# Attention and a feed-forward layer on one core: the last span's second product in two levels of Strassen

## Chip, core and metric

The kernel runs on one core of a Trainium2 chip. The metric is device time in microseconds (us). It is the median of three runs; the profile comes from one further execution of the same kernel. TensorE is called PE in the profile, VectorE DVE, ScalarE ACT, GpSimd POOL, and SyncE, which only issues transfers here, SP.

## What is computed

Cut to what matters:

```python
def reference(q, k, v, g_q, g_k, w_in, w_out):      # q, k, v: 8 x 12 x 448 x 64
    q_n, k_n = rmsnorm(q, g_q), rmsnorm(k, g_k)
    attn = softmax(q_n @ k_n.T / 8)                  # per batch and head
    x = (attn @ v), heads side by side               # 3584 x 768
    h = x @ w_in                                     # 768 x 2048
    g = np.maximum(h, 0.0) ** 2
    return g @ w_out                                 # 2048 x 768, result 3584 x 768
```

The change lies in the last line alone, and there in its last quarter of tokens.

## The kernel before

The 3584 tokens are worked off in four spans (`NSPAN = 4`) of 896 tokens, two batches of `S = 448` each. For every span the kernel does the attention, then a first product (x by w_in, then the squared ReLU), then a second product (by w_out). Both products use one level of Strassen's method in Winograd's form: operands are cut into 2 x 2 blocks, and seven block products (named A11, S2, S1, S3, A12, A22, S4 after their weight operand) take the place of eight. The seven weight operands of each product are made once, at the start, and kept in device memory as `w1s` and `w2s`. The sums of activations are `xC` (from `xT`) for the first product and `gC` (from `gT`) for the second; `combine` (L1021 to L1032) makes the latter on DVE.

`first_product` (L1034) goes over `HF = 8` row blocks f of w_in's columns, and for each over the seven block products. One block product is three matmul statements of 128 x 128 weights by 128 x 448 activations (L1068). Four PSUM tiles receive them: `pa` (from the pool `ps_s`), and `pb`, `pc`, `pd` from the function `bank` (L460), which hands out two PSUM banks "m" and "n" in turn, by a counter `turn`. DVE adds L1075 (z), L1078 (y) and L1083 (into `gT`) and the ACT and POOL steps L1040 and L1044 empty them.

`second_product` (L1091) goes over `HC = 3` column blocks m and the seven block products i, in the order of `uses2` (L642). One block product is eight matmul statements of 128 x 448 (L1134). Results leave by `deliver` (L1102): a DVE transpose in 32 x 32 squares (L1104), then four transfers (L1107). The very last block product is done by `last_block` (L1109), in two halves of 224 columns (L1119), so that the end of the kernel is short. Before each second product `turn` is moved on by one, so that its first bank is not the one that the first product has used last.

Weights come as a stream. `load_blocks(upto)` (L651) issues one transfer for each weight block on the SP queue (L665), into five buffers `sw`; it is called with "my index + 5", so up to four blocks lie ahead of the one in use. A block of the first product has 192 KB and serves 3 matmul statements; a block of the second product has 256 KB and serves 4. The stream runs on across the products and spans. SP does its issues in program order, and waits in that order too: for a buffer to become free, and, at `deliver`, for DVE's transpose.

The order of each engine's work is the order of the program text; it is written out by hand (`manual_schedule`), and there is no planner. In the spans before the last, the attention of the next span is woven into the second product. In the last span there is no attention left: first product and second product follow each other, with nothing else on PE.

In the profile every float32 matmul statement shows as two weight loads and two matmul records.

Of the kernel before, what the change touches and what calls it, by code (L numbers as in the profile page):

```python
# [10 lines left out]
F32 = mybir.dt.float32  # L11
U32 = mybir.dt.uint32
AF = mybir.ActivationFunctionType
ALU = mybir.AluOpType
# [373 lines left out]
def attention_then_ffn_bounded(  # L388
# [47 lines left out]
    HF = NFC // 2  # L436
    NSPAN = B // 2
# [7 lines left out]
    def start_of(span):  # L445
        return 2 * span * NPAIR
# [8 lines left out]
    ps_s = ctx.enter_context(tc.tile_pool(name="ps_s", bufs=2, space=bass.MemoryType.PSUM))  # L455
    ps_o = ctx.enter_context(tc.tile_pool(name="ps_o", bufs=1, space=bass.MemoryType.PSUM))
# [29 lines left out]
    HW = HC * P  # L486
# [153 lines left out]
    stream = []  # L640

    uses2 = [(m, i) for m in range(HC) for i in (A11, A12)]  # L642
    uses2 += [(m, i) for m in range(HC) for i in (S2, S1, S3, A22, S4)]
    def order_of(span, f):

        return (A11, A12, S2, S1, S3, A22, S4) if span == f == 0 else range(7)

    N1 = HF * 7
    N2 = HC * 7 * (HF // 4)

    def load_blocks(upto):  # L651

        while len(stream) < min(upto, NSPAN * (N1 + N2)):
            n = len(stream) % (N1 + N2)
            if written[0] < min(2 * (n // 7 + 1) if n < N1 else 2 * NFC, 2 * NFC):
                return
            sw = loads.tile([P, 4, P], F32, tag="sw", name="sw", bufs=5)
            if n < N1:
                sw = sw[:, 0:HC]
                src = w1s[n // 7, order_of(len(stream) // (N1 + N2), n // 7)[n % 7]].rearrange("p (c m) -> p c m", c=HC)  # L660
            else:
                n -= N1
                m, i = uses2[n // (HF // 4)]
                src = w2s[i, n % (HF // 4), :, :, m * P:(m + 1) * P]
            nc.sync.dma_start(sw, src)  # L665
            stream.append(sw)
# [4 lines left out]
    places, halves, rests = [], [], {}  # L671
# [419 lines left out]
    def second_product(work, span):  # L1091

        B11, B21, B22 = gT[:, 0:HF, 0:S], gT[:, HF:, 0:S], gT[:, HF:, S:2 * S]
        T1, T2, T4, T3 = gC[:, 0], gC[:, 1], gC[:, 2], gT[:, 0:HF, S:2 * S]
        rhs_of = {A11: B11, S2: T2, S1: T1, S3: T3, A12: B21, A22: T4, S4: B22}
        rows = out.rearrange("(b g t) n -> b t g n", b=B, t=32)
        n = span * (N1 + N2) + N1
        add = nc.vector.tensor_tensor
        done = []
        turn[0] += 1  # L1100

        def deliver(ct, col, t, queues=(nc.sync,), part=slice(0, S // 32)):  # L1102
            osb = work.tile([P, S // 32, 32], F32, tag="osb", name="osb")[:, part]
            nc.vector.transpose(osb.rearrange("p g n -> p (g n)"), ct[:, part.start * 32:part.stop * 32])  # L1104
            for i in range(0, P, 32):
                queue = queues[i // 32 % len(queues)]
                queue.dma_start(rows[2 * span + t, :, part, col * P + i:col * P + i + 32], osb[i:i + 32])  # L1107

        def last_block(n, m):  # L1109

            deliver(*done.pop(), (nc.sync, nc.scalar))
            load_blocks(n + 5)
            rhs = rhs_of[S4]
            ct = work.tile([P, S], F32, tag="ct", name="ct", bufs=1)
            half = S // 64 * 32
            for part in (slice(0, half), slice(half, S)):
                ps = bank("ps")[:, part]
                for c in range(HF):
                    nc.tensor.matmul(ps, stream[n + c // 4][:, c % 4], rhs[:, c, part],  # L1119
                                     start=c == 0, stop=c == HF - 1)  # L1120
                add(ct[:, part], y[:, part], ps, ALU.add)
                deliver(ct, m, 1, (nc.sync, nc.scalar), slice(part.start // 32, part.stop // 32))

        p1s, c11s = {}, {}
        for j, (m, i) in enumerate(uses2):
            if span == NSPAN - 1 and j == len(uses2) - 1:
                last_block(n, m)
                break  # L1130
            ps = bank("ps")
            for c in range(HF):
                load_blocks(n + 5)
                nc.tensor.matmul(ps, stream[n][:, c % 4], rhs_of[i][:, c], start=c == 0, stop=c == HF - 1)  # L1134
                n += c % 4 == 3
                if c == HF // 2 - 1 and done:
                    yield
                    deliver(*done.pop())
                if span == 0 and j < 8 and c % 4 == 1:
                    combine(j % 4 * HF // 4 + c // 4, (j // 4,))  # L1140
                if c < HF - 1:
                    yield
            if i == A11:
                p1s[m] = work.tile([P, S], F32, tag="p1", name="p1", bufs=HC)
                nc.scalar.copy(p1s[m], ps)
            elif i == S2:
                add(p1s[m], p1s[m], ps, ALU.add)
            elif i == S1:
                y = work.tile([P, S], F32, tag="y", name="y", bufs=1)
                add(y, p1s[m], ps, ALU.add)  # L1150
            else:
                ct = work.tile([P, S], F32, tag="ct", name="ct", bufs=1)
                add(ct, p1s[m] if i in (A12, A22) else y, ps, ALU.add)
                if i == S3:
                    add(p1s[m], p1s[m], ps, ALU.add)
                done.append((ct, m + (HC if i in (S3, A22) else 0), 1 if i in (S3, S4) else 0))
            yield
        if done:
            deliver(*done.pop())
            yield  # L1160


    load_v(0)

    def ahead(u, nxt):

        if u == 7 * (HF - 3):
            norm(nxt)
        if u == 7 * (HF - 2):
            norm(nxt + 1)  # L1170
            load(nxt + 2)
        if u == 7 * (HF - 1):
            transposes(nxt)
            squares(nxt + 2)

    with tc.tile_pool(name="words", bufs=2) as spare["pool"]:
# [20 lines left out]
        with tc.tile_pool(name="first_product", bufs=2, reuse_waits="tile") as work:  # L1197
            for u, _ in enumerate(first_product(work, 0)):
                if u == 6:

                    left = ps_s.tile([P, 2, 512], F32, tag="s", name="bits")
# [4 lines left out]
                if u == N1 - 4:  # L1206
                    transposes(NAT)
                    squares(NAT + 2)
    for span in range(NSPAN):
        more = span + 1 < NSPAN  # L1210
        nxt = start_of(span + 1)
        if span:
            with tc.tile_pool(name="first_product", bufs=2, reuse_waits="tile") as work:
                for u, _ in enumerate(first_product(work, span)):
                    if more:
                        ahead(u, nxt)
        with tc.tile_pool(name="second_product", bufs=2, reuse_waits="tile") as work:
            rest = second_product(work, span)
            if more:
                places_for(work, NJ)  # L1220
                places.append(qkT[:, 1])
                halves[:] = [work.tile([P, 2, S // 2], F32, tag=f"half{m}", name="half", bufs=1) for m in range(2)]
                sums_for(work)
                total, done, most = HC * (7 * HF + 4) - 20, 0, 10 * NPAIR + 1
                for u, _ in enumerate(attention(nxt)):
                    while done < total * min(u + 1, most) // most + 3 * max(u + 1 - most, 0):
                        next(rest)
                        done += 1
            for _ in rest:
                pass  # L1230


@with_exitstack
# [85 lines left out]
```

## Time and profile before

| what | value |
|---|---|
| median of three runs | 1363.46 us (1362.93 to 1364.74) |
| the profiled execution's own time | 1362.31 us |
| span of the profiled execution, first to last instruction | 1360.5 us |
| mean granted clock of TensorE | 0.997 |
| busy: PE, DVE, POOL, ACT | 1340.5, 832.1, 566.0, 430.0 us |
| last span: first product on PE | from 1101.5 to 1227.8 us |
| last span: second product on PE | from 1227.8 to 1354.3 us |

The profile has a page of summaries and views of the trace: groups of instructions (count, busy time, mean duration, idle time before them and what ended it), the chain of work that ended last, a timeline of one stretch, a table by windows, and, for one source line, the time from a transfer's issue to its landing. In a timeline, records that follow each other with the same names are merged, and their number stands as "x6"; times are from the span's start.

### The profile page before, as it was taken

Reading aid. Unit: us, or ns where it says so; the run is one execution under the profiler, and the core shown is the slowest. Engines: PE = TensorE matmul, PEld = TensorE weight load, DVE = VectorE, ACT = ScalarE, POOL = GpSimd, SP = SyncE. Lnnn points to the kernel's source line nnn. Section 1 sums busy time; section 2 is a strip of 40 time slices with the busy share of each in tenths; the row PEclk is TensorE's granted clock in tenths of the full one; section 3 lists DMA queues with packets and bytes.
Section 4 is the critical chain, followed back from the end, with each engine's and each line's share of the span. In section 5 each row is a group of like instructions: output and inputs, shape, how many; then the busy total and the mean of one; then the engine's idle time right before and its main releaser. Section 6 shows DMA issues by size and latency. Waiting matters only on the chain.

```text
span 1360.5 us, 16880 instructions
## 1 busy us (share of the span) xinstructions
PE 1340.5 (99%) x5618; PEld 641.6 (47%) x5618; DVE 832.1 (61%) x1482; ACT 430.0 (32%) x674; POOL 566.0 (42%) x458
## 2 busy tenths in 40 slices
PE   8999999999999999999999999999999999999998
PEld 3333445444444455444444455444444455555554
DVE  6999788599987333467778523557788633332111
ACT  7886466433332011233332111233333211110000
POOL 5667533466563122655565222446566312220000
PEclk9999999999999999999999999999999999999999
DMA  9777999655685333355675433345765443334443
GB/s 240 208 229 198 314 360 327 183 130 111 130 151 129 99 87 88 100 119 118 135 150 115 113 100 87 101 104 118 142 129 110 105 103 87 87 91 107 106 111 71
DMA packets 434084, 190.12 MB, mean 140 GB/s; under 512 B 282948, under 2 KB 430788, under 8 KB 433988
## 3 DMA queue, kind: packets, MB, share of 16 engines
q1 hardware_dynamic: 427364, 180.33, 52.2%
q0 software_dynamic: 4736, 8.40, 2.5%
q8 instruction: 47, 0.77, 0.2%
q10 hardware_dynamic: 1888, 0.23, 0.1%
q14 instruction: 49, 0.40, 0.1%
HBM read 155.72 MB, written 33.16 MB: 139 GB/s over the span
## 4 chain that ended last, share of the span: by engine, by line
PE 90%; DVE 5%; ACT 3%; DMA 1%; issue 1%; SPq 0%; POOL 0%; ACTq 0%; DVEq 0%
PE ps L1134 37%; PE pd L1068 10%; PE pa L1068 10%; PE pc L1068 10%; PE sc L785 7%; PE pav L862 7%; PE pb L1068 5%; ACT gT L797 1%; DVE gT L810 1%; DVE rstd L715 1%; PE sc L793 1%; DVE gC L613 1%; PE tot L876 1%; DMA gT<-in_moe_w_in_dram 1%; PE pav L851 1%
## 5 line engine op out<-in xcount | busy, mean ns | idle before, releaser
L1134 PE MATMUL ps<-gT,sw 128*128 128x448 f32 x752 | 293.0, 543 | 0.0
L1134 PE MATMUL ps<-gC,sw 128*128 128x448 f32 x576 | 225.2, 543 | 0.0
L1044 POOL TENSOR_TENSOR gT<-gT 128x448 f32<-128x448 f32 x96 | 93.9, 980 | 283.3 <-ACT gT L1040 283.3
L1134 PEld LDWEIGHTS ps<-gT,sw 128*128 128x128 f32 x752 | 141.1, 190 | 146.4 <-issue 142.0
L750 POOL TENSOR_TENSOR half<-half,mhalf 128x28 f32<-128x28 f32 x36 | 175.2, 4868 | 72.7 <-DVE half L749 69.2
L1134 PEld LDWEIGHTS ps<-gC,sw 128*128 128x128 f32 x576 | 108.1, 190 | 112.9 <-issue 110.7
L1068 PE MATMUL pa<-xT,sw 128*128 128x448 f32 x384 | 155.0, 540 | 0.6 <-ACT p L1072 0.6
L1040 ACT ACTIVATE gT<-gT 128x448 f32<-128x448 f32 x96 | 55.3, 577 | 311.2 <-DVE gT L1083 311.2
L787 ACT ACTIVATE pr<-sc 128x896 f32<-128x896 f32 x87 | 77.5, 915 | 121.7 <-PE sc L785 121.7
L785 PE MATMUL sc<-qkT 64*64 64x448 f32 (+1 forms) x1152 | 109.8, 496 | 0.0
L1068 PEld LDWEIGHTS pa<-xT,sw 128*128 128x128 f32 x384 | 72.9, 190 | 72.6 <-issue 70.7
L583 POOL TENSOR_TENSOR gC<-gC 128x384 f32<-128x384 f32 x64 | 76.2, 1209 | 62.2 <-DVE gC L579 60.4
L1083 DVE TENSOR_TENSOR gT<-z,pd 128x448 f32<-128x448 f32 x32 | 19.8, 620 | 97.8 <-PE pd L1068 97.6
L1068 PE MATMUL pd<-xT,sw 128*128 128x448 f32 x192 | 77.9, 542 | 1.3 <-DVE z L1075 1.3
L1068 PE MATMUL pd<-xC,sw 128*128 128x448 f32 x192 | 77.5, 540 | 1.3 <-DVE gT L1083 1.3
L1068 PE MATMUL pb<-xC,sw 128*128 128x448 f32 x192 | 77.5, 540 | 0.1
L752 POOL TENSOR_TENSOR qk<-qk,half 128x448 f32<-128x448 f32 x72 | 76.4, 1081 | 2.8
L1068 PE MATMUL pc<-xC,sw 128*128 128x448 f32 x192 | 77.4, 539 | 0.0
L1068 PE MATMUL pc<-xT,sw 128*128 128x448 f32 x192 | 77.4, 539 | 0.0
L830 POOL DMA_DIRECT2D xT<-factors x72 | 38.0, 532 | 94.7 <-DMA factors<-square 63.9
L862 PE MATMUL pav<-pr,vt 64*64 64x448 f32 x348 | 72.7, 537 | 0.0
L862 PE MATMUL rest<-pr,vt 64*64 64x448 f32 x348 | 72.7, 537 | 0.0
(144 smaller groups left out, 1849.6 us busy)
## 6 DMA issues: line engine op xcount, KB each, us to landing
sw<-w1s SPq DMA_DIRECT2D x224, 192.0 KB, 2.4
sw<-w2s SPq DMA_DIRECT2D x168, 256.0 KB, 3.2
w1s<-gC SPq DMA_DIRECT2D x8, 1344.0 KB, 6.4
w2s<-gC SPq DMA_DIRECT2D x8, 1344.0 KB, 6.1
out_dram<-osb SPq DMA_DIRECT2D x186, 56.0 KB, 1.9
qk<-in_q_dram SPq DMA_DIRECT2D x144, 56.0 KB, 3.5
qk<-in_k_dram SPq DMA_DIRECT2D x144, 56.0 KB, 3.0
xT<-factors POOLq DMA_DIRECT2D x72, 112.0 KB, 3.4
```

The lines of the kernel that those rows point to most:

```text
L583: nc.gpsimd.tensor_tensor(*[blocks_of(n)[:, place_of(n, i)] for i in (dst, x, y)], op)
L750: nc.gpsimd.tensor_tensor(half, half, mhalf, ALU.pow)
L752: nc.gpsimd.tensor_tensor(qkn[:, s], raw[:, s], half[:, s * NG:(s + 1) * NG].rearrange("p g -> p g ()").to_broadcast([P, NG, 32]), ALU.mult)
L785: nc.tensor.matmul(sc[part, h, 0:n], qkT[rows, 0, 1, keys], qkT[rows, 0, 0, of], start=True, stop=True)
L787: nc.scalar.activation(pr, sc[:, :, 0:n], AF.Exp)
L830: nc.gpsimd.dma_start(xT[h * D:(h + 1) * D, b % 2, hp], sums["out"][i % 2].rearrange("(h g) t -> h () (g t)", h=2)[h].to_broadcast([D, S]))
L862: nc.tensor.matmul(into, vs[i][rows, h, c, :], probs[i, c][rows, h, :], start=(c == 0), stop=(c == NF), skip_group_check=True)
L1040: nc.scalar.activation(g, src, AF.Relu)
L1044: nc.gpsimd.tensor_tensor(g, g, g, ALU.mult)
L1068: nc.tensor.matmul(ps, stream[n + at][:, c], rhs[:, c], start=first and c == 0, stop=c == HC - 1, skip_group_check=not first)
L1083: add(g, x, ps, ALU.add)
L1134: nc.tensor.matmul(ps, stream[n][:, c % 4], rhs_of[i][:, c], start=c == 0, stop=c == HF - 1)
```

## The change

The first three spans are as before. The last span's second product is done by a new function, `last_product`, that

- goes over the seven block products in the order A11, A12, S2, S1, S3, A22, S4 on the outside, and treats all three column blocks of one before it goes to the next;
- cuts each of them for the column blocks m = 0 and 1 (of both halves of the result: four of its six) once more into 2 x 2 parts, and does seven inner block products of four matmul statements each, 128 x 128 by 128 x 224; the third column block stays with eight statements of 128 x 448 (`third`);
- gets the sums of weight parts from GpSimd (`add_weights`: four additions of 128 x 512 for each outer step) and the sums of activations from DVE (`add_g`: four subtractions of 128 x 896);
- adds the inner results up by `meet` (DVE, 128 x 224) and `based` (GpSimd, 128 x 224, which adds to z and y what the result already holds);
- loads the weights of one outer step by one transfer of 1536 KB into one of two places (`load_set`): the first two at the start of the last span, the others at the end of each step. The stream of small blocks ends with the last span's first product;
- keeps its sums in places whose contents are no longer needed (`qk`, `qkT`, `xT`, `xC`, and parts of `gT`), and one new tile `wb`;
- does not move `turn` on before it begins.

`deliver` is moved out of `second_product`; `last_block` is gone, and the last `third` is done in two halves in its place.

The core of the diff:

```diff
-        while len(stream) < min(upto, NSPAN * (N1 + N2)):
+        while len(stream) < min(upto, NSPAN * (N1 + N2) - N2):
...
+        def load_set(o):
+            if o < len(order):
+                nc.sync.dma_start(sets[o % 2].rearrange("p (k e) -> p k e", k=2),
+                                  w2s[order[o]].rearrange("k p c m -> p k (c m)"))
...
+            for dst, x, y, op in ((s1, a21, a22, add), (s2, s1, a11, sub), (s3, a11, a21, sub), (s4, a12, s2, sub)):
+                nc.gpsimd.tensor_tensor(dst, x, y, op)
...
+            dst, x, y = ((t1, b12, b11), (t2, b22, t1), (t3, b22, b12), (t4, b21, t2))[n]
+            nc.vector.tensor_tensor(dst, x, y, sub)
...
+        def run(ps, lhs, rhs, first=True):
+            for c in range(HK):
+                nc.tensor.matmul(ps, lhs[:, c], rhs[:, c], start=first and c == 0, stop=c == HK - 1,
+                                 skip_group_check=not first)
...
+            into = {A11: [(None, p1s)], A12: [(p1s, None)], S2: [(p1s, p1s)], S1: [(p1s, ys)],
+                    S3: [(ys, None), (p1s, p1s)], A22: [(p1s, None)], S4: [(ys, None)]}[i]
...
+            def third():
+                m = HC - 1
+                for part in (slice(0, HS), slice(HS, S)) if end else (slice(0, S),):
+                    ps = bank("ps")[:, part]
+                    for c in range(HF):
+                        nc.tensor.matmul(ps, weights_of(o, m, c // HK)[:, c % HK], rhs_of[i][:, c, part],
+                                         start=c == 0, stop=c == HF - 1)
...
+                if not end:
+                    add_g(o + 1, 0)
+                    send(m)
...
+            pa = ps_s.tile([P, 2, 512], F32, tag="s", name="pa")[:, 0, 0:HS]
+            run(pa, a11, b11)
+            p1 = small_of("p1i")
+            nc.scalar.copy(p1, pa)
+            if not end:
+                third()
+            pb = ps_o.tile([P, S], F32, tag="o", name="pb")[:, 0:HS]
+            run(pb, s2, t2)
+            z, y = small_of("zi"), small_of("yi")
+            nc.vector.tensor_tensor(z, p1, pb, add)
+            z21, z12 = based(1, 0, z, "za"), based(0, 1, z, "zb")
+            pc = bank("pc")[:, 0:HS]
+            run(pc, s1, t1)
+            nc.vector.tensor_tensor(y, z, pc, add)
+            add_g(o + 1, 1)
+            y22 = based(1, 1, y, "yb")
+            pd = ps_o.tile([P, S], F32, tag="t", name="pd")[:, 0:HS]
+            run(pd, s3, t3)
+            meet(1, 1, y22, pd)
+            run(pa, a12, b21, False)
...
+            add_g(o + 1, 2)
+            run(pd, a22, t4, False)
+            meet(1, 0, z21, pd)
+            send(1)
+            run(pc, s4, b22, False)
+            meet(0, 1, z12, pc)
+            send(0)
+            add_g(o + 1, 3)
+            load_set(o + 2)
+            add_weights(o + 1)
+            if end:
+                third()
...
+        load_set(0)
+        load_set(1)
+        with tc.tile_pool(name="first_product", bufs=2, reuse_waits="tile") as work:
+            for u, _ in enumerate(first_product(work, NSPAN - 1)):
+                if u == N1 // 2:
+                    add_weights(0)
+                if u == N1 - 2:
+                    for n in range(4):
+                        add_g(0, n)
+        with tc.tile_pool(name="second_product", bufs=2, reuse_waits="tile") as work:
+            rest.send(work)
```

More of the change, by code (lines that the diff above doesn't have):

```diff
@@ L1095, in second_product @@
         rhs_of = {A11: B11, S2: T2, S1: T1, S3: T3, A12: B21, A22: T4, S4: B22}
-        rows = out.rearrange("(b g t) n -> b t g n", b=B, t=32)
         n = span * (N1 + N2) + N1
@@ L1100, in second_product @@
         turn[0] += 1
[L1102 to L1126, printed above, removed]
+        p1s = {}
         for j, (m, i) in enumerate(uses2):
-            if span == NSPAN - 1 and j == len(uses2) - 1:
-                last_block(n, m)
-                break
             ps = bank("ps")
@@ L1137, in second_product @@
                     yield
-                    deliver(*done.pop())
+                    deliver(work, span, *done.pop())
                 if span == 0 and j < 8 and c % 4 == 1:
@@ L1158, in second_product, with deliver @@
         if done:
-            deliver(*done.pop())
+            deliver(work, span, *done.pop())
             yield
+    rows = out.rearrange("(b g t) n -> b t g n", b=B, t=32)
+    def deliver(work, span, ct, col, t, queues=(nc.sync,), part=slice(0, S // 32)):
+        osb = work.tile([P, S // 32, 32], F32, tag="osb", name="osb")[:, part]
+        nc.vector.transpose(osb.rearrange("p g n -> p (g n)"), ct[:, part.start * 32:part.stop * 32])
+        for i in range(0, P, 32):
+            queue = queues[i // 32 % len(queues)]
+            queue.dma_start(rows[2 * span + t, :, part, col * P + i:col * P + i + 32], osb[i:i + 32])
@@ new lines, in last_product, with weights_of, sums_of, add_weights @@
+    def last_product(pool):
+        rhs_of = {A11: gT[:, 0:HF, 0:S], S2: gC[:, 1], S1: gC[:, 0], S3: gT[:, 0:HF, S:2 * S],
+                  A12: gT[:, HF:, 0:S], A22: gC[:, 2], S4: gT[:, HF:, S:2 * S]}
+        order = (A11, A12, S2, S1, S3, A22, S4)
+        HK, HS = HF // 2, S // 2
+        qf, tf, xf, cf = (t.rearrange(f"{ax} -> p ({ax[2:]})") for t, ax in (
+            (qk, "p n e"), (qkT, "p a s n"), (xT, "p b h n"), (xC, "p i h n")))
+        NS, NW2, NT2 = HK * P, 2 * HK * HW, HK * HS
+        wb = pool.tile([P, NW2], F32, tag="wb", name="wb", bufs=1)
+        sets = [(w[:, 0:NW2]) for w in (qf, wb)]
+        left = [[qf[:, NW2:NW2 + NS], qf[:, NW2 + NS:NW2 + 2 * NS], tf[:, 0:NS], tf[:, NS:2 * NS]],
+                [xf[:, 4 * NT2 + n * NS:4 * NT2 + (n + 1) * NS] for n in range(3)] + [tf[:, 2 * NS:3 * NS]]]
+        ts = [[t[:, n * NT2:(n + 1) * NT2].rearrange("p (c n) -> p c n", c=HK) for n in range(4)] for t in (cf, xf)]
+        dead = [gT[:, f, 0:S] for f in range(HF)]
+        used = [0]
+        sub, add = ALU.subtract, ALU.add
+        def weights_of(o, m, k):
+            return sets[o % 2].rearrange("p (k c n) -> p k c n", k=2, c=HK)[:, k, :, m * P:(m + 1) * P]
+        def sums_of(o):
+            return [t.rearrange("p (c n) -> p c n", c=HK) for t in left[o % 2]]
+        def load_set(o):
+            if o < len(order):
+                nc.sync.dma_start(sets[o % 2].rearrange("p (k e) -> p k e", k=2),
+                                  w2s[order[o]].rearrange("k p c m -> p k (c m)"))
+        def add_weights(o):
+            if o == len(order):
+                return
+            s1, s2, s3, s4 = sums_of(o)
+            (a11, a12), (a21, a22) = [[weights_of(o, m, k) for k in range(2)] for m in range(2)]
+            for dst, x, y, op in ((s1, a21, a22, add), (s2, s1, a11, sub), (s3, a11, a21, sub), (s4, a12, s2, sub)):
+                nc.gpsimd.tensor_tensor(dst, x, y, op)
+        def parts_of(o):
+            rhs = rhs_of[order[o]]
+            return [[rhs[:, k * HK:(k + 1) * HK, t * HS:(t + 1) * HS] for t in range(2)] for k in range(2)]
+        def add_g(o, n):
+            if o == len(order):
+                return
+            (b11, b12), (b21, b22) = parts_of(o)
+            t1, t2, t3, t4 = ts[o % 2]
+            dst, x, y = ((t1, b12, b11), (t2, b22, t1), (t3, b22, b12), (t4, b21, t2))[n]
+            nc.vector.tensor_tensor(dst, x, y, sub)
+        def small_of(name):
+            return work.tile([P, HS], F32, tag=name, name=name, bufs=1)
+        work = yield load_set, add_weights, add_g
+        p1s = [work.tile([P, S], F32, tag="p1", name="p1", bufs=HC) for _ in range(HC)]
+        ys = dead[0:HC]
+        def place():
+            used[0] += 1
+            return dead[HC + used[0] % (HF - HC)]
+        def run(ps, lhs, rhs, first=True):
+            for c in range(HK):
+                nc.tensor.matmul(ps, lhs[:, c], rhs[:, c], start=first and c == 0, stop=c == HK - 1,
+                                 skip_group_check=not first)
+        for o, i in enumerate(order):
+            end = o + 1 == len(order)
+            (b11, b12), (b21, b22) = parts_of(o)
+            (a11, a12), (a21, a22) = [[weights_of(o, m, k) for k in range(2)] for m in range(2)]
+            s1, s2, s3, s4 = sums_of(o)
+            t1, t2, t3, t4 = ts[o % 2]
+            into = {A11: [(None, p1s)], A12: [(p1s, None)], S2: [(p1s, p1s)], S1: [(p1s, ys)],
+                    S3: [(ys, None), (p1s, p1s)], A22: [(p1s, None)], S4: [(ys, None)]}[i]
+            leaves = any(dst is None for _, dst in into)
+            into = [(base, dst or [place() for _ in range(HC)]) for base, dst in into]
+            at = ((HC if i in (S3, A22) else 0), 1 if i in (S3, S4) else 0)
+            def send(m, queues=(nc.sync,)):
+                if leaves:
+                    deliver(work, NSPAN - 1, into[0][1][m], m + at[0], at[1], queues)
+            def third():
[5 more added lines that the diff above has]
+                                         start=c == 0, stop=c == HF - 1)
+                    for base, dst in into:
+                        if base is None:
+                            nc.scalar.copy(dst[m][:, part], ps)
+                        else:
+                            nc.vector.tensor_tensor(dst[m][:, part], base[m][:, part], ps, add)
+                    if end:
+                        deliver(work, NSPAN - 1, into[0][1][m], m + at[0], at[1], (nc.sync, nc.scalar),
+                                slice(part.start // 32, part.stop // 32))
+                if not end:
+                    add_g(o + 1, 0)
+                    send(m)
+            def meet(m, t, x, ps):
+                part = slice(t * HS, (t + 1) * HS)
+                for (base, dst), left in zip(into, x):
+                    nc.vector.tensor_tensor(dst[m][:, part], left, ps, add)
+            def based(m, t, x, name):
+                part = slice(t * HS, (t + 1) * HS)
+                all = []
+                for n, (base, _) in enumerate(into):
+                    if base is None:
+                        all.append(x)
+                        continue
+                    all.append(small_of(f"{name}{n}"))
+                    nc.gpsimd.tensor_tensor(all[-1], x, base[m][:, part], add)
+                return all
+            pa = ps_s.tile([P, 2, 512], F32, tag="s", name="pa")[:, 0, 0:HS]
[18 more added lines that the diff above has]
+            run(pa, a12, b21, False)
+            if into[0][0] is None:
+                nc.scalar.copy(into[0][1][0][:, 0:HS], pa)
+            else:
+                meet(0, 0, [base[0][:, 0:HS] for base, _ in into], pa)
+            add_g(o + 1, 2)
[8 more added lines that the diff above has]
+            add_weights(o + 1)
+            if end:
+                third()
+        yield
@@ L1208, in attention_then_ffn_bounded @@
                     squares(NAT + 2)
-    for span in range(NSPAN):
-        more = span + 1 < NSPAN
+    for span in range(NSPAN - 1):
         nxt = start_of(span + 1)
@@ L1214, in attention_then_ffn_bounded @@
                 for u, _ in enumerate(first_product(work, span)):
-                    if more:
-                        ahead(u, nxt)
+                    ahead(u, nxt)
         with tc.tile_pool(name="second_product", bufs=2, reuse_waits="tile") as work:
             rest = second_product(work, span)
[L1219 to L1228, printed above, removed]
+            places_for(work, NJ)
+            places.append(qkT[:, 1])
+            halves[:] = [work.tile([P, 2, S // 2], F32, tag=f"half{m}", name="half", bufs=1) for m in range(2)]
+            sums_for(work)
+            total, done, most = HC * (7 * HF + 4) - 20, 0, 10 * NPAIR + 1
+            for u, _ in enumerate(attention(nxt)):
+                while done < total * min(u + 1, most) // most + 3 * max(u + 1 - most, 0):
+                    next(rest)
+                    done += 1
             for _ in rest:
                 pass
+    with tc.tile_pool(name="last_product", bufs=2, reuse_waits="tile") as last:
+        rest = last_product(last)
+        load_set, add_weights, add_g = next(rest)
+        load_set(0)
[9 more added lines that the diff above has]
+            rest.send(work)
 @with_exitstack
```

## Prediction

> **What bounds the kernel now.** I read the chain of work that ended last first, for the last span. It is PE alone:
>
> ```profile
> 1225.71 2.25 PE pc L1068 x6
> 1227.97 120.27 PE ps L1134 x320
> 1348.23 6.07 PE ps L1119 x32
> 1354.30 0.02 issue
> 1354.32 0.40 DVE ct L1121
> ```
>
> So a matmul saved here is time saved, and any wait of PE is time lost. A float32 statement is two records. 448 columns cost 120.27 / 320 = 0.3758 us a record, 0.7516 a statement; 224 columns cost 6.07 / 32 = 0.1897 a record, 0.3794 a statement. The groups of this stretch say what limits the narrow ones:
>
> ```profile
> L1119 PE MATMUL ps<-gT,sw 128*128 128x224 f32 x32 | 6.2, 353 | 0.0
> L1119 PEld LDWEIGHTS ps<-gT,sw 128*128 128x128 f32 x32 | 6.1, 190 | 0.4 <-issue 0.4
> ```
>
> A weight load takes 190 ns and the loads are busy for 6.1 of 6.2 us: 224 columns just cover their weight load, and cost 1% more than half of 448.
>
> Next, the timeline where the last span begins, because the change puts two transfers there:
>
> ```profile
> 1103.05 1.88 SPq L1107 DMA_DIRECT2D out_dram<-osb  x4
> 1105.03 6.02 SPq L665 DMA_DIRECT2D sw<-w1s  x5
> 1110.54 1.67 PE L1068 MATMUL pa<-xT,sw 128*128 128x448 f32 x4
> ```
>
> SP waits for the old span's last result, sends it, and only then, at 1105.03, issues block 4 of the new span (blocks 0 to 3 are already on the way). PE takes block 4 up at 1110.54. That is all the cover there is: 5.5 us.
>
> What a large transfer does to a small one behind it, from the views of L598 and L665 at 222.7 and 223.1 us:
>
> ```profile
> L598 SPq DMA_DIRECT2D w2s<-gC x1: 371/371/371, 222.7 to 222.7; - x1
> DMA to landing us min/median/max: 6.0/6.0/6.0
> L665 SPq DMA_DIRECT2D sw<-w1s x1: 513/513/513, 223.1 to 223.1; - x1
> DMA to landing us min/median/max: 6.2/6.2/6.2
> ```
>
> A 192 KB block needs 2.3 us in this kernel (median landing of this group in the last 260 us). Behind 1344 KB it needs 6.2: it landed after the big one.
>
> Then DVE at the seam of the two products:
>
> ```profile
> 1225.75 0.62 DVE L1083 TENSOR_TENSOR gT<-z,pd 128x448 f32<-128x448 f32 x1 [3.89 <-PE pd L1068]
> 1226.29 0.62 DVE L1031 TENSOR_TENSOR gC<-gT,gC 128x448 f32<-128x448 f32 x1
> 1226.82 0.62 DVE L1032 TENSOR_TENSOR gT<-gT 128x448 f32<-128x448 f32 x1
> 1228.00 0.62 DVE L1083 TENSOR_TENSOR gT<-z,pc 128x448 f32<-128x448 f32 x1 [0.56 <-PE pc L1068]
> ```
>
> The last of these empties the bank of `pc`, 0.2 us after PE has filled it.
>
> Last, the table by windows after the one long gap of PE (2.23 us, ended at 21.64):
>
> ```profile
> 21.50:22.00 0.50, 0.36 (x3) 0.36 (x4) 0.50 (x2) 0.50 (x2) 0.48 (x1) 0.85 1.08 342
> 22.00:22.50 0.50, 0.50 (x5) 0.22 (x3) 0.50 (x2) 0.50 (x1) 0.00 (x0) 0.50 1.10 350
> 25.50:26.00 0.50, 0.50 (x6) 0.27 (x6) 0.50 (x2) 0.50 (x2) 0.14 (x1) 1.00 1.21 369
> ```
>
> The third number from the end is the granted clock, the last one GB/s. After 2.2 us of idling the clock is halved from about 21.7 to 25.2 us.
>
> [...]the trace shows 342 to 350 at 20 to 25 us, while weights are read. [...]the square L1044 takes 0.93 us alone and 1.17 beside L1032.
>
> **The change, part by part.**
>
> *Matmuls.* Of 21 block products, 14 (m = 0 and 1) go from 14 x 8 = 112 wide statements, 112 x 0.7516 = 84.2 us, to 7 x 7 x 4 = 196 narrow ones, 196 x 0.3794 = 74.4 us. Gain 9.8 us, all on the chain. The other seven cost what they did, the last in halves as before.
>
> *The first two sets, at the start of the span.* They wait for nothing new: their places' last readers are attention's, long done, and SP has just waited for DVE anyway. But they stand ahead of block 4 on SP's queue: 2 x 1.573 = 3.146 MB. With 350 GB/s they take 9.0 us, block 4 itself 0.6, and what a transfer needs beside its bytes is about 1.7 (2.3 less 0.6); 1105.0 + 11.3 = 1116.3, and some 0.2 more for the issues[...]. PE needs block 4 at 1110.5: a stall of 6.0 us. Behind PE nothing else can run; the other engines wait for it. Bounds: with the 425 GB/s of the best slice in the view of transfers from 200 to 300 us 4.1 us; with 245 GB/s (192 KB in 2.3 us against 768 KB of L540 in 4.7) 9.8. Blocks 5 to 8 follow in 0.6 us each, so it happens once. [...]1.7 more (1.0 to 1.8).
>
> *The seam.* `turn` isn't moved on, so step A11's `third` takes the bank that comes after `pd`: that of `pc`, the first product's last. In the built program its first matmul waits for the DVE addition that empties `pc`. Ahead of that addition on DVE now stand four `add_g`: 128 x 896, 1.06 us each (row L810, `acc<-acc,pr`, 1064 ns). They start when L1032 is through, 1227.4, and end at 1231.7; the addition ends at 1232.4. PE is there after `pa` of step A11: 1227.8 + 4 x 0.3794 = 1229.3. Stall 3.1 us; 2.5 to 4.0[...]. Queued behind it is all of PE. After 3.1 us I count the halved clock again, 1.7 (0 to 1.7[...]).
>
> *An outer step.* PE: 28 x 0.3794 + 8 x 0.7516 = 16.6 us. DVE: four `add_g` 4.3; z, y and four `meet` of 224 columns at 0.39 (L1121); `third` 0.62; three transposes of 0.64 where results leave: 4.3 + 2.3 + 0.6 + 1.9 = 9.1; S3, which has two targets, 4.3 + 3.9 + 1.2 + 1.9 = 11.3. POOL: four sums of 512 columns, 0.93 x 512 / 448 = 1.06 each, and three `based` of 224 columns, about 0.5 each (0.47 to 0.93: the trace has no such width): 5.8; S3 7.3. All fit into 16.6, so only order counts. The narrow point is `pd`: its second use must wait for `meet(1,1)`, this for `yb`, this for y and the POOL queue. From the end of `third`: PE wants `pd` again after 4 x 1.52 = 6.1. One target: z at 3.0, y at 3.65, `yb` behind `add_g` (4.7) at 5.2, `meet` at 5.65. In time by 0.4. S3: DVE's two additions, `add_g` and transpose end at 3.15, z at 3.55, y at 4.0; POOL has six `based`; [...]it ends at 7.1 to 7.5, the second `meet` at 7.5 to 8.0. Stall 1.1 to 2.0, I take 1.5 (0.5 to 2.5).
>
> *At no cost.* `add_weights` of step o + 1 runs on POOL from `yb` of step o on, 4.3 us, and is wanted some 11 us after; `add_weights(0)` in the first product has 60 us. A set is issued at a step's end and wanted 16.6 us later; one alone takes 1.7 + 4.5 = 6.2. If that cover were gone the difference would be PE's. ACT's copies (below 0.53 each) have `third`'s 6.0 us. The output transfers are as many as before. The tail has the same two halves, addition 0.39 and transpose 0.41.
>
> *Sum.* -9.8 + 6.0 + 1.7 + 3.1 + 1.7 + 1.5 = +4.2 us. Span 1360.5 + 4.2 = 1364.7; with the 1.8 us around the span (1362.31 - 1360.5) 1366.5. The median of the runs is 1.15 above that execution: **1367.7 us**.
>
> **Rivals.**
> - *Faster: the sets don't hold the stream up*[...]. Place: block 4 at 1110.54; price: 7.7 us return, -3.5, 1360.0. The point: the rest of the sum is -3.5, so stall and clock loss together may be 3.5 us; with 1.7 for the clock, a landing before 1112.3 decides for a gain. Against: the 6.2 us behind L598. If the seam is free too: 1353.6.
> - *The same losses at their low ends*: 4.1 + 1.0 + 2.5 + 0 + 0.5 = 8.1, less than 9.8: 1361.8, no difference that can be told.
> - *The step becomes the bound*: [...]in each of the six steps with a base, 1.06 less the 0.4 of slack in five of them, and 1.06 in S3: 4.4 more, 1372. [...]Against: DVE and POOL are busy only 55% and 35% of a step.
>
> **How the numbers follow.** A measurement of this kernel tells about 0.2%, 2.7 us, from no change. Forecast 0.47 (its own range 1364.5 to 1371); step-bound 0.15; low ends 0.22; stream not held 0.13, seam free as well 0.03. Slower 0.62, same 0.22, faster 0.16. The range goes from 1360.0 (stream not held) to 1374 (step-bound with a slow stream); outside it lie the free seam and half of the cases at either rim, about 0.15.
>
> **What would show it.** PE idle for about 6 us before the last span's fifth block (`pa`, around 1110), with a transfer as releaser, and half clock after it; PE idle about 3 us before the first `third`, released by DVE; 1 to 2 us before S3's second `pd`; narrow records at 0.19 us. Wrong would be: no gap at 1110, gaps in each step, or narrow records that cost more than 0.195.

## The result and the profile after

| | before | after |
|---|---|---|
| median of six runs | 1362.93 us (1361.46 to 1364.74) | 1368.97 us (1367.49 to 1371.44) |
| the profiled execution's own time | 1362.31 us | 1369.9 us |
| its span | 1360.5 us | 1368.0 us |
| mean granted clock of TensorE | 0.997 | 0.993 |
| first product of the last span, on PE | 126.28 us | 133.88 us (1100.29 to 1234.17) |
| second product, on PE | 126.49 us | 127.28 us (1234.17 to 1361.45) |
| from PE's last matmul to the end | 6.21 us | 6.55 us |

The ratio after to before is 1.0046 (95% interval 1.0032 to 1.0059): 6.0 us slower. The forecast was 1367.7 us.

Where does it go? In the waits of PE over the last 368 us of the changed kernel (total us, times, longest) only three lines are more than issue gaps, and none of them is in the kernel before:

```profile
PE pa L1068 <- DMA sw<-w1s: 5.2, 1, 5.2
PE ps L1232 <- DVE gT L1083: 3.5, 1, 3.5
PE pd L1207 <- DVE p L1250: 2.1, 1, 2.1
```

These are the sets' wait, the wait at the seam and the wait in S3. The chain of work that ended last shows what each leaves behind it (start, length, what; dots stand for other lines):

```profile
1104.84 9.74 DMA sw<-w1s
1114.71 4.62 PE pa L1068 x6
...
1235.65 3.10 DVE xC L1191 x3
...
1239.34 9.22 PE ps L1232 x16
...
1323.22 2.82 PE pd L1207 x8
```

Read the records after each wait against their like elsewhere in the same chain: six wide records take 2.25 us and here 4.62; sixteen take 6.01 and here 9.22; eight narrow ones take 1.51 and here 2.82. The eight after these (2.16 us) are slow too. So PE lost a further 2.37, 3.21 and, with 2.82 + 2.16 for 3.02, 1.96 us behind the waits. The trace's record of the granted clock accounts for 2.15, 2.98 and 1.71 of them, 6.84 in all; the rest, some 0.2 us each, comes with a wait at full clock too (in the chain of the run `bank_spread` eight narrow records behind a wait of 2.1 us took 1.78 us in place of 1.51, and those after them 1.51). The table by windows shows the first of these: from left the stretch, PE, PEld, DVE, ACT, POOL, then the granted clock, the transfers' share and GB/s.

```profile
1110.00:1112.00 2.00, 0.00 (x0) 0.00 (x0) 0.14 (x1) 0.58 (x1) 0.93 (x1) 1.00 1.01 424
1116.00:1118.00 2.00, 2.00 (x4) 0.85 (x3) 0.00 (x0) 0.00 (x0) 0.00 (x0) 0.50 0.00 2
1120.00:1122.00 2.00, 2.00 (x7) 1.06 (x6) 0.37 (x1) 0.00 (x0) 0.92 (x1) 1.00 0.37 98
```

PE idles while the transfer engines are full (share 1.01, 424 GB/s), then works at clock 0.50 from 1114.71 to 1119.0 with nothing left to wait for, then at 1.00.

SP's side of it, in the timeline (start, length, queue, line):

```profile
1103.82 0.42 SPq L1170 DMA_DIRECT2D qk<-w2s  x1
1104.33 0.41 SPq L1170 DMA_DIRECT2D wb<-w2s  x1
1104.84 28.38 SPq L665 DMA_DIRECT2D sw<-w1s  x12
```

The two sets stand ahead of the fifth block (the first of the x12), which took 9.74 us to land where 192 KB take 2.3 elsewhere. Their own issues also put it off by 1.0 us: it leaves 4.54 us after the first matmul of the span, in the kernel before 3.51.

The seam, where before showed DVE's addition from `pc` 0.2 us behind PE:

```profile
1233.73 1.82 DVE L1191 TENSOR_TENSOR xC<-gT 128x896 f32<-128x896 f32 x1
...
1238.67 0.61 DVE L1083 TENSOR_TENSOR gT<-z,pc 128x448 f32<-128x448 f32 x1
...
1242.67 1.57 DVE L1029 TENSOR_TENSOR gC<-gT,gC 128x448 f32<-128x448 f32 x1
```

The addition now comes 4.5 us after PE's last matmul into `pc` (1234.17), behind four `add_g`, of which the first took 1.82 us beside the square L1044 and the others 1.08 to 1.09. After it the last four sums of `gC` take 1.57 to 1.70 us where they took 0.62; POOL's four sums of 512 columns run at the same time. That slowdown costs nothing here, because PE is late already; it will matter in an experiment.

And S3's second `pd`:

```profile
1318.77 1.51 POOL L1260 TENSOR_TENSOR za<-zi,p 128x224 f32<-128x224 f32 x1
...
1322.09 0.65 POOL L1260 TENSOR_TENSOR yb<-yi,p 128x224 f32<-128x224 f32 x1
...
1322.77 0.39 DVE L1250 TENSOR_TENSOR p<-yb,pd 128x224 f32<-128x224 f32 x1 [0.23 <-POOL yb L1260]
```

POOL makes six `based` of 0.65 us in a row, the second 1.51 long, beside DVE's `add_g` (1318.49 to 1319.77); the last `meet` ends at 1323.16, and PE follows at 1323.22.

By these starts the last span is 7.60 + 0.79 + 0.34 = 8.7 us longer, and what lies ahead of it 1.2 us shorter (1100.29 against 1101.52, the same instructions): together the 7.5 us between the spans. The medians say 6.0: the profiled execution of after is 0.9 above its median and that of before 0.6 below. The 1.2 us go back to the clock as well: before's profile has half clock from 21.85 to 25.26 us, which costs 1.7, and after's has none there. Of all eleven profiles of this case four show it, and in them the last span starts at 1101.2 to 1101.7 us, in the other seven at 1099.4 to 1100.3.

### The profile page after: what moved, and what is told of

The parts are those of the page before. It is cut to its first block, busy times and chain, and to the rows that moved or that the text cites. A ratio compares the mean times of both kernels' runs of the same rounds, so it can differ in the third digit from the quotient of the medians.

```text
span 1368.0 us, 17269 instructions
## 1 busy us (share of the span) xinstructions
PE 1337.3 (98%) x5786; PEld 675.0 (49%) x5786; DVE 876.0 (64%) x1541; ACT 431.2 (32%) x680; POOL 624.3 (46%) x507
## 4 chain that ended last, share of the span: by engine, by line
PE 86%; DVE 6%; ACT 3%; DMA 2%; issue 1%; POOL 1%; SPq 0%; DVEq 0%; ACTq 0%
PE ps L1106 28%; PE pa L1068 10%; PE pd L1068 9%; PE pc L1068 9%; PE sc L785 7%; PE pav L862 7%; PE pb L1068 5%; PE ps L1232 3%; PE pd L1207 2%; ACT gT L797 1%; PE pc L1207 1%; PE pa L1207 1%; DMA sw<-w1s 1%; DVE gT L810 1%; DVE rstd L715 1%
## 5 line engine op out<-in xcount | busy, mean ns | idle before, releaser
L1044 POOL TENSOR_TENSOR gT<-gT 128x448 f32<-128x448 f32 x96 | 94.4, 985 | 294.1 <-ACT gT L1040 294.1
L1106 PE MATMUL ps<-gT,sw 128*128 128x448 f32 x576 | 225.8, 543 | 0.0
L1106 PE MATMUL ps<-gC,sw 128*128 128x448 f32 x432 | 170.1, 543 | 0.0
L1106 PEld LDWEIGHTS ps<-gT,sw 128*128 128x128 f32 x576 | 107.5, 190 | 113.9 <-issue 110.3
L1106 PEld LDWEIGHTS ps<-gC,sw 128*128 128x128 f32 x432 | 80.6, 190 | 86.3 <-issue 83.4
```

The costliest lines, as they stand in the source:

```text
L1044: nc.gpsimd.tensor_tensor(g, g, g, ALU.mult)
```

## The experiments

My theory: four things, the sets ahead of block 4, the bank at the seam, S3's six additions, and the clock that each wait may cost, make the loss; without them the matmul gain of 9.8 us stands. The rivals: the step as a whole is too tight, so that waits only move; or the clock is lost in any case. Each ratio below is against the kernel before on the same chip.

**The bank.** `turn` is moved on, as before each second product of the other spans.

```diff
         work = yield load_set, add_weights, add_g
+        turn[0] += 1
```

> The bank counter is moved on by one before the last product, nothing else. Theory (three waits of PE, each followed by half clock, are the whole loss; before plus 6.0 us): the wait of the first wide block product for DVE (3.5 us) and the half clock after it (3.2 us) go, 1369.0 - 6.7 = 1362.3. But DVE's queue behind it is no shorter: from the changed profile, z of step A11 should then stand behind the late gC sums (1.6 us each beside GpSimd) until about 1248 on that profile's clock, so a new wait of 2 to 3 us before that step's second pd is likely, with or without half clock: 1362 to 1367, most likely 1365. Rival (the seam wait is DVE being late in any case, not the bank): no change, 1369, with PE waiting elsewhere for as long.

Measured: 1367.26 us (1366.48 to 1368.15), ratio 1.0033 (1.0020 to 1.0046). It came out above what I expected. The wait at the seam is gone, but another has come, in PE's waits:

```profile
PE pa L1068 <- DMA sw<-w1s: 5.5, 1, 5.5
PE pd L1208 <- DVE p L1251: 4.8, 2, 2.7
```

Twice 2.1 to 2.7 at `pd`: the one is S3's, the other is new, in step A11. DVE's timeline says why:

```profile
1242.30 1.57 DVE L1029 TENSOR_TENSOR gC<-gT,gC 128x448 f32<-128x448 f32 x1
...
1248.04 0.37 DVE L1273 TENSOR_TENSOR zi<-p1i,pb 128x224 f32<-128x224 f32 x1
```

The step's z waits behind `add_g` and behind four `gC` sums that take 1.57 to 1.70 us beside POOL's sums. So the bank was the seam's cause, but only its first: DVE's backlog of some 10 us is the second, and it takes 2.7 of the 3.5 us back. The profile shows this; the medians of this kernel and of after lie 1.7 us apart, and the intervals of their ratios overlap.

**The sets, three ways.** First in sixteen pieces of 192 KB, each behind every third block of the first product's stream:

```diff
+        def load_piece(t):
+            o, k, c = t // 8, t // 4 % 2, t % 4
+            dst = sets[o].rearrange("p (k c m) -> p k c m", k=2, c=HK)[:, k, c]
+            nc.sync.dma_start(dst, w2s[order[o], k, :, c])
...
-        load_set(0)
-        load_set(1)
...
+                if u % 3 == 1 and u < 48:
+                    load_piece(u // 3)
```

> The first two weight sets come in sixteen pieces of 192 KB, one for every third block of the last span's first product, in place of two transfers of 1536 KB ahead of its fifth block. Theory: the fifth block no longer waits, so 5.2 us of stall and 2.4 us of half clock go: 1369.0 - 7.6 = 1361.4, and no gap of PE in the first product. Rival (the stall comes from the bytes as such, or from SP's own waits, and is only paid in small change): the stream falls behind at several blocks, total gain under 3 us.

Measured: 1361.8 us (1357.31 to 1363.97, 13 runs), ratio 0.9991 (0.9982 to 1.0000). In the profile the first product takes 126.28 us, to the hundredth what it took before; the waits at the seam and in S3 stand unchanged. The median is 7.2 us below after's, and only these two transfers' place has changed: 5.2 us for the wait, 2.4 for the clock behind it in after's profile.

Then from ScalarE's queue, whole, at the same time:

```diff
-        load_set(0)
-        load_set(1)
...
+                if u == 0:
+                    load_set(0, nc.scalar)
+                    load_set(1, nc.scalar)
```

> The first two sets are issued from ScalarE's queue just after the first block product, about 0.4 us earlier than now; the stream stays on SP's queue. Theory ([...]the fifth block stands behind both sets in one queue): with two queues the fifth block lands beside the sets, within about 4 us, before 1110.5: no stall, 1361.4, or a small one at one of the following blocks, up to 1363. Rival (it is bandwidth: 3.1 MB must go first whatever the queue): stall stays within 1 us of 5.2, 1369.

Measured: 1362.24 us (1360.1 to 1366.6, 14 runs), ratio 1.0000 (0.9991 to 1.0008). PE still waits for the fifth block, though briefly:

```profile
1110.58 2.49 PE L1068 MATMUL pa<-xT,sw 128*128 128x448 f32 x6 [1.22 <-DMA sw<-w1s]
```

The same 3.1 MB hold the block up by 1.2 us from another queue and by 5.2 from the same. This profile is the fastest of the 14 runs, and the two cases differ in more than the queue:

```profile
1103.45 0.39 ACTq L1170 DMA_DIRECT2D qk<-w2s  x1
1103.69 9.73 SPq L665 DMA_DIRECT2D sw<-w1s  x6
1103.91 0.46 ACTq L1170 DMA_DIRECT2D wb<-w2s  x1
```

Of the 4.0 us, 1.0 is that SP no longer issues the sets first, and the fifth block now leaves between them. It landed after 6.76 us, not within the 4 that I expected. The next block tells the queues apart: it left after both sets (1104.21) and landed at 1112.84, while packets of the sets ran until 1114.78; in after's profile the block behind the fifth landed at 1115.10, after both. So here the place in the queue made most of the wait, and the issues (1.0 us) and the sets' bytes beside the block (the 1.2 us left) the smaller part.

Last, still on SP, but behind the fifth block instead of ahead of it:

```diff
-        load_set(0)
-        load_set(1)
...
+                if u == 0:
+                    load_set(0)
+                    load_set(1)
```

> The two sets are issued as they are, on SP's queue, but one block later: behind the fifth block of the first product and ahead of the sixth. Theory[...]: the fifth block lands in time; the sixth lands some 0.6 us after the fifth does now, 1115.2 on the clock of the changed kernel's profile, and is wanted 2.25 us later than the fifth, at 1111.7: a gap of 3.0 to 3.8 us instead of 5.2, and half clock with it or not: 1366 to 1368. Rival (something at the fifth block itself is late): no gap or the same gap.

Measured: 1367.94 us (1364.58 to 1368.74), ratio 1.0039 (1.0026 to 1.0052). In PE's waits:

```profile
PE pd L1068 <- DMA sw<-w1s: 3.2, 1, 3.2
```

The wait moves to the sixth block and is 2.0 us shorter, near the 2.25 us of one block product by which that block is wanted later. This profile is the fastest of the five runs; the ratio hardly differs from after's (1.0046). Here moving the sets by one place in the queue moved the wait with them, from the fifth block (5.2 us) to the sixth (3.2).

**The wait at the seam, filled.** Nine narrow statements more, whose results nobody reads, let PE work through the wait:

```diff
+            if o == 0:
+                idle = ps_o.tile([P, S], F32, tag="t", name="idle")[:, 0:HS]
+                for _ in range(9):
+                    nc.tensor.matmul(idle, a11[:, 0], b11[:, 0], start=True, stop=True)
             if not end:
                 third()
```

> Nine extra narrow matmul statements (3.4 us) into a bank that nobody reads stand between the first narrow block product and the first wide one of the last product, where PE idles for 3.5 us. They add work and remove no wait. Theory (the gap halves the clock afterwards): the wait stays, its 3.2 us of half clock go, 1369.0 - 3.2 = 1365.8. Rival (the first wide block product is slow for another reason, its operands or GpSimd beside it): 1369 or more, 16 records still in 9.2 us.

Measured: 1369.01 us (1366.29 to 1369.08), ratio 1.0040 (1.0027 to 1.0053). In the profile the half clock after the seam is gone, and the second product is 124.32 us, 2.96 shorter than after's. But the median isn't lower than that of after, so the 1365.8 that I expected did not come. The profile shows where the time went: this execution lost 1.7 us to the clock near 22 us, long before the change, and starts its last span 0.9 later; the wait behind the sets (5.65) and the loss behind it (2.76) are 0.8 longer together, and the end 0.3. That leaves 0.9 between the two profiles. With such differences between single executions the medians of five and six runs decide nothing here; a later run asks the same with fewer other waits.

**S3.** DVE adds y and `pd` into a small tile, and GpSimd adds that to the two targets, so that `pd` comes free without waiting for POOL:

```diff
+                x22 = small_of("xi")
+                nc.vector.tensor_tensor(x22, y, pd, add)
+                for base, dst in into:
+                    nc.gpsimd.tensor_tensor(dst[1][:, HS:S], x22, base[1][:, HS:S], add)
```

> In step S3 alone, DVE first adds y and pd into a small tile, which frees pd; GpSimd then adds this to the two targets. Before, GpSimd made both bases first and pd waited for them. Theory (the GpSimd queue is late for pd in S3 alone): the gap of 2.1 us goes, and the half clock that followed it in one of three profiles, 0 to 2 us: 1369.0 less 2 to 4, 1366. Rival (DVE and GpSimd are the bound of the step, not the order): the gap moves to a later wait of the same step, 1369.

Measured: 1366.69 us (1363.8 to 1368.01), ratio 1.0029 (1.0019 to 1.0040): 2.3 us below after, with intervals that overlap. (The expectation says that half clock followed this wait in one of three profiles; in the five profiles of that time it had followed in four.) S3's wait is gone from the profile, the clock stays at 1.00 there, and no other wait comes. (The wait behind the sets was 7.0 us in this execution.) POOL has as many additions as before in this step and DVE one fewer, so the wait was the order of additions, not POOL's load.

**Bank and pieces together.**

> The bank counter is moved on and the first two sets come in sixteen pieces. Theory: the two edits act at different places and add up: 1361.8 (pieces alone) less the 1.7 that the counter gave alone, 1360.1; the gap of about 2.7 us before the second pd of step A11 stays. Rival (the waits shift into each other): no more than the pieces alone, 1361.8.

Measured: 1361.47 us (1357.38 to 1363.45, 22 runs), ratio 0.9984 (0.9976 to 0.9992). The runs fall into two groups, with none between 1359.99 and 1361.10: ten from 1357.38 to 1359.99, twelve from 1361.10 to 1363.45. Their medians lie 4.1 us apart. The profiled execution is of the upper one (1362.07), and its PE has this in step A11:

```profile
1244.32 3.35 PE L1213 MATMUL pd<-xC,qk 128*128 128x224 f32 x8 [2.73 <-DVE p L1256]
1247.46 3.16 PE L1213 MATMUL pc<-gT,qkT 128*128 128x224 f32 x8
```

From the first start to the next `pa` (1250.45) these sixteen records take 6.13 us; at full clock they take 3.03. That is 3.1 us, most of the distance of the groups. This execution also has the 1.7 us near 22 us. The mean granted clock parts the groups too: 0.994 to 0.996 in the upper, 0.996 to 0.999 in the lower. The guess: the same wait of 2.7 us halves the clock in some executions and not in others.

**That guess, tried.** The same kernel, with seven useless narrow statements (2.66 us) where the wait is:

```diff
             run(pa, a12, b21, False)
+            if o == 0:
+                idle = ps_s.tile([P, 2, 512], F32, tag="s", name="idle")[:, 0, 0:HS]
+                for _ in range(7):
+                    nc.tensor.matmul(idle, a11[:, 0], b11[:, 0], start=True, stop=True)
```

> The kernel with the counter moved on and the sets in pieces has one gap of 2.7 us before the second pd of step A11, and its times fall into two groups, 1357.4 to 1360.0 and 1361.1 to 1363.5. Here seven extra narrow statements (2.66 us) into a bank that nobody reads fill that gap; the wait itself stays. Theory (the upper group is the runs in which the gap was followed by half clock): the upper group goes, all runs between 1357 and 1360.5, median near 1358.5. Rival (the two groups have another cause, such as the stream of transfers): both groups stay, median 1361.5.

Measured: 1358.59 us (1356.75 to 1360.04, 10 runs), ratio 0.9974 (0.9964 to 0.9983). None of ten runs lies in the upper group, where 12 of 22 did (less the 0.8 us by which this chip is faster, it would begin at 1360.3). PE in its profile:

```profile
1239.50 2.81 PE L1292 MATMUL idle<-gT,qk 128*128 128x224 f32 x14
1242.33 1.78 PE L1213 MATMUL pd<-xC,qk 128*128 128x224 f32 x8
```

Useless work took the place of idling and the next records are quick. The median is 2.9 us lower; 0.8 of it is the chip (the kernel before had 1361.92 there, 1362.74 on the other), and the two ratios' intervals overlap by a little. It is the missing group that shows the cause.

**All of it mended.** Counter, pieces and S3's addition of above, and the order of DVE's sums at the seam: one `add_g` earlier, and two ahead of the last `combine`, so that the late `gC` sums and the bank's addition stand where they are wanted. The last result leaves by two queues.

```diff
-                if u == N1 - 2:
-                    for n in range(4):
-                        add_g(0, n)
+                if u == N1 - 5:
+                    add_g(0, 0)
+                if u == N1 - 2:
+                    add_g(0, 1)
...
                 if span and f == HF - 1 and i == S4:
+                    ahead_of_last()
                     combine(f)
```

Here `ahead_of_last` calls `add_g(0, 2)` and `add_g(0, 3)`.

> All mends together: counter moved on, sets in pieces, S3 by the direct addition, the sums of activations for the first step issued in the order in which they are wanted (the last two just ahead of the last gC sums), and the last step's final result on two queues. The same result is computed. Theory (the matmul gain of 9.8 us was there all the time, under three waits and their half clock): no gap of PE in the last span, second product 126.5 - 9.8 = 116.7 us, total 1363.0 - 9.8 = 1353.2. Rival (the narrow steps have a cost of their own that the waits now hide): second product over 119 us, total 1356 or more.

Measured: 1352.97 us (1351.62 to 1354.84), ratio 0.9926 (0.9913 to 0.9939): 9.8 us faster than the kernel before on the same chip and, by the two ratios, 1.2% faster than the changed one. In the last span one wait is left on PE:

```profile
PE pd L1214 <- DVE p L1257: 0.5, 1, 0.5
```

The second product takes 117.34 us, the first 126.28. So the first rival falls: the steps have room for their DVE and POOL work. The second falls too: in the last span no clock is lost. That the medians differ by just 9.8 is partly chance: by the profiles the last span is 8.0 us shorter, because its part after PE's last matmul is 1.2 longer.

## Why the prediction was right, and where its sizes were off

The sum, term by term, against the profile of the changed kernel:

| term of the sum | forecast, us | profile, us |
|---|---|---|
| narrow matmuls | -9.8 | -10.0 |
| wait for the block behind the sets | +6.0 | +5.23 |
| lost behind it (half clock) | +1.7 | +2.37 |
| wait at the seam | +3.1 | +3.49 |
| lost behind it (half clock) | +1.7 | +3.21 |
| wait in S3 | +1.5 | +2.11 |
| lost behind it (half clock) | not counted | +1.96 |
| tail | 0 | +0.34 |
| sum | +4.2 | +8.7 |

The -10.0 is what is left of the second product without its waits and losses (127.28 - 10.77 against 126.49). The part ahead of the last span takes 1.2 us off, which no term forecast.

- *Matmuls: right.* Eight narrow records take 1.51 us, 0.189 each, and 392 of them 74.1 where the wide ones took 84.2. The mended kernel confirms the term by itself: 117.34 less its 0.54 of wait is 116.8, against 126.49, or -9.7.
- *The sets: right in place and kind, 0.8 too long.* I let 3.34 MB come at 350 GB/s, 11.5 us from the first set's issue to the fifth block's landing. It took 10.75 (1103.82 to 1114.57); less the 1.7 us that the prediction estimates beside the bytes that is some 370 GB/s. Once the sets flow a window shows 424, about the 425 that the forecast's lower bound had used.
- *The seam: right.* The bank of `pc`, behind four `add_g`, as forecast; 3.49 in place of 3.1 because the first took 1.82 us, beside the square L1044. What I did not see is what stands behind it: the `gC` sums of 0.62 us took 1.57 to 1.70 beside POOL's sums, so moving `turn` on, the plain remedy, brings only 1.7 us by the medians.
- *S3: right in place, 0.6 too small.* The term that was mis-sized is the narrow `based`: 0.65 us each, not 0.5, so six make 0.9 more, of which the rest of that sum, too high, takes 0.3 back. POOL's sums of 512 columns were too cheap as well (1.27 us alone, not 1.06), at no cost here.
- *The clock: the step that failed in size.* I counted two losses of 1.7 us: an estimate from the one stretch at half speed that the trace of before had (some 3.5 us in the table, 3.41 by the record of the clock). The profile has three, of 6.84 us by the record of the clock (7.5 with what follows any wait). The losses here were not of one size: behind the sets and behind the seam the half clock lasted 6.83 us, twice one stretch; see below. That S3's 2.1 us could cost it I had not counted at all, though the trace of before showed 2.2 us to be enough.
- *The chances.* The medians say +6.0, the profiled execution +7.5; the forecast's +4.2 with 1.15 for the median gave 1367.7, 1.3 under the measured median. That it came so close is in part luck. The three waits were off by -0.8, +0.4 and +0.6 us and added up to 10.8 where I had 10.6; the clock's share was too small by some 4 us in the profile; 1.2 us ahead of the last span made up for some of it; and the typical run loses less clock than the profiled one (mean granted clock 0.993 there, 0.995 in the three fastest of the six runs, 0.991 in the slowest).
- *The rivals.* "The sets don't hold the stream up" was wrong for one queue, and nearly right for two (1.2 us). "The step becomes the bound" was wrong, and its 4.4 us were an estimate of mine: beside the seam no step but S3 made PE wait, and the mended kernel has 0.54 us in all seven. "Low ends" was wrong: no wait lay at its low end. One figure doesn't follow from its own terms: without the sets' 7.7 us and the seam's 4.8 the sum gives 1355.2; the 1353.6 of the prediction needs S3's 1.5 away too.
- *The tail: not free.* In each of the ten profiles of changed kernels it is longer than before's 6.21 us, by 0.3 to 1.3. In nine of them DVE's last transpose waits 0.3 to 0.7 us for output transfers (in the mended one, with two queues, it doesn't), and in all ten SP's last issue takes 0.6 to 1.6 us where it took 0.45.

Left open: why those issues take longer, and what the half clock at the seam costs in the median.

## What to carry to other kernels

A prefetch for later is not free because its data are wanted late: look at what stands behind it in its own queue, and cut it into pieces as small as that neighbour (here the wait of 5.2 us was gone), or give it another queue (here 1.2 us were left). Where a wait is removed, ask what the engine that was waited for still has in front of it; the next item may bring most of the wait back (here 2.7 us of 3.5). In the profiles of this case an idle gap of PE of 2.1 us and more cost up to 3.1 us on top of its length for the clock, by where the gap fell (nothing in the cheapest case, 3.07 in `bank_spread`); no interval with 1.84 us of idling or less, as counted below, cost any.

## What the runs showed of the hardware

- *The clock after a gap went by where the gap fell.* Up to the last matmul the clock's record shows half clock only for 3.41, 6.83 or 10.24 us at a time (the last behind the wait of 7.0 us in `s3_direct`, where the mean clock from 1100 to 1130 us is 0.83). Its changes stand at 21.850 and 25.263 us in the trace of before, and at 1112.184, 1119.011, 1238.477, 1245.304, 1323.810 and 1327.223 us in that of after: within each trace whole multiples of 3.4133 us apart, to 1 ns. Counted from the span's start, this grid lies 1.37 us behind whole multiples in before, 2.85 in after. I added up PE's idle time in each interval of the grid, from the start of the clock's record (4.8 us in before, 6.3 in after). In these two profiles intervals at full clock with 2.23 us of idling (before) and 2.71, 2.63 and 2.11 (after) ended in half clock, and none with 1.44 us or less did; at half clock, intervals with no idling ended in full clock, and those with 2.53 and 0.86 didn't. Over all eleven profiles, at full clock each of the 18 intervals with 1.92 us or more ended in half clock, and none with 1.84 or less did; at half clock, those with at most 0.08 ended in full clock, and those with 0.69 or more didn't. So in these profiles a gap cost when some 1.9 us of it fell into one interval.
- *So gaps of one length cost different sums.* Of the gaps in the last span, those of 5.2 to 7.0 us lost 2.15 to 3.05 us by the record, every time (four). Five of 3.5 us lost 2.98, three times 1.71, and nothing; one of 3.2 nothing; two of 2.7 lost 3.07 and nothing; of eight of 2.1 five lost 1.71 and three nothing. From the two figures 1.9 and 3.41 I estimate that a gap of 2.1 us costs in half of all cases, one of 2.7 in two thirds, and one of more than 3.8 always. The two groups of run times of `bank_spread`, 4.1 us apart, agree with such a draw. In after the three losses took 6.84 of 1368 us, more than the whole of what the change lost (6.0).
- *A second queue was worth more than the time to issue.* In `sets_actq` the issues that SP no longer makes were worth 1.0 us, and the wait fell by 4.0, from 5.2 to 1.2; a block issued after both sets landed 1.9 us before their last packet. The fifth block is still late, and its queue gets a sixth of the bytes: from 1106 to 1112 us SP's queue, in packets (the pieces in which a transfer moves) of 1.5 KB, moved 0.39 MB and ScalarE's, in packets of 6 KB, 2.04 MB.
- *DVE and POOL.* Where both add at the same time, in after's last span: DVE's additions of 448 columns went from 0.62 us to 1.57 to 1.70 beside POOL's sums, those of 896 from 1.08 to up to 2.12; POOL's of 512 columns took 1.26 to 1.30 at best and up to 2.15 beside DVE's.
